# Filter tiles between kv tiles, and halves of filter tiles between gates, in the opening of a long-convolution and GeGLU kernel

## The chip, the cores and the metric

The kernel runs on one core of a Trainium2 chip. The metric is the device time of one execution in microseconds (us), lower is better. The engines are named as in the profile: PE is TensorE's matmul side and PEld its weight loads, DVE is VectorE, ACT is ScalarE, POOL is GpSimd and SP is SyncE, which here only issues DMAs.

## The reference

Two layers are applied twice in turn, A, B, A, B, to one sequence of 2048 tokens with 576 channels, in bfloat16. Layer A is a gated long convolution, layer B a gated feed-forward network of width 4608.

```
def A(q, k, v, shift_k, ssm_k, ssm_D):         # q is layernorm(x)
    k_shift = sum over t of k_pad[:, t:t+S] * shift_k[:, ks-1-t]      # 4 taps
    kv = k_shift * v
    y = irfft(rfft(kv, 2S) * rfft(ssm_k, 2S))[:S] + kv * ssm_D        # causal convolution, length 2048
    return q * y

def B(x, w_gate, w_up, w_down):                # x is layernorm(x)
    return (gelu(x @ w_gate) * (x @ w_up)) @ w_down

x = A_q
x = x + A(layernorm(x), ...);  x = x + B(layernorm(x), ...)
x = x + A(layernorm(x), ...);  x = x + B(layernorm(x), ...)
```

The convolution does not depend on x, so its result y is computed once and used by both A layers.

## The kernel before

**Tiling.** The sequence is cut into four blocks of 512 tokens, the channels stay together. Each block b of the filter `ssm_k` (transposed to time by channels, `hT[b]`) goes through a Fourier transform that is written as matmuls with the matrix `G`: four tiles `kt` of 128 frequencies, each with two halves `s` (cosine and sine). `h_tile(b, kt, pool)` makes one such tile: `fwd_h` runs eight matmuls of 128x288 per half into a PSUM tile, ScalarE evacuates it (L189), and the finished tile is spilled to DRAM (`Hd[b][kt]`, L266) by a DMA on POOL's queue. Block 1's tiles go to a resident tensor `H1`, and are spilled too. The kv blocks are transformed in the same way with the matrix `F1`: in the opening, `kfwd(kt)` makes the kv tile `kc[kt]` of block 0 (L198, L200), `kacc(kt)` multiplies it with block 0's filter tile on VectorE (L225 to L229), `pair0` adds and subtracts those products (L630), and `inv0(mt)` transforms back (L261), which gives `y[0]`.

**The opening** is the function `begin`: one order written out by hand for all engines, from the first DMA to the first gate/up matmul of the feed-forward network. After block 0's `inv0` it runs layer A's gate for the first 512 tokens, in four row groups j: `gate0(j)` is two VectorE operations (L801, L806), a small POOL operation for minus the mean (`nm`, L834) and a square with a sum on ScalarE (`junk`, L842); `root0(j)` makes 1/sqrt(variance) in two POOL operations (`ve` L849, `rstd` L850); `norm0(j)` writes the normalised tile xn on VectorE (L1017, L1019); `turn0(j)` transposes it with nine TensorE operations into PSUM (L1028); `copy0(j)` copies it to `xnT` on VectorE (L1036). Between these stand the remaining filter tiles of blocks 2 and 3, and `kv1_ops(n)`, VectorE's multiplies for block 1's kv.

**Queues and buffers in the opening.** The transposed filters `hT[b]` come by transposing DMAs on SP's queue (`load_h`, L495) into a pool of two buffers, so `load_h(3)` waits for the last reader of `hT[1]`, which is `h_tile(1, 3)`. On SP's queue the first two gate/up weight groups (`more(1)`, L760 to L762) stand ahead of `load_h(3)`, and the third (`more(2)`) behind it. POOL's queue carries the spills, the loads of k and v (`load_k`, `load_v`) and the small gate operations, in program order. A spill is not issued at once: `spill` puts it in a list, and `flush` issues what stands in the list, so a tile's spill goes out when the next tile is flushed. `ps()` hands out PSUM tiles: three buffers shared with the feed-forward network and with `turn0`, and every fourth time a buffer of its own.

**Behind the opening** an order worked out when the kernel is built interleaves everything else: gate/up matmuls (L1116), GeLU on ScalarE (L1120), the product hT on VectorE (L1121), down matmuls (L1132), and blocks 1 to 3 of the convolution in between. It does not depend on the order inside `begin`.

Of the kernel before, what the change touches and what calls it, by code (L numbers as in the profile page):

```python
# [14 lines left out]
BF16 = mybir.dt.bfloat16  # L15
# [3 lines left out]
P = 128  # L19
# [37 lines left out]
class Conv:  # L57
# [418 lines left out]
    def begin(self, gate0, root0, norm0, turn0, copy0, x0_stats, more, scratch, wide, stay):  # L476

        tc, nc, D = self.tc, self.nc, self.D
        with ExitStack() as es:
# [13 lines left out]
            def load_h(b):  # L493
                t = hp.tile([P, RT, D], BF16, tag="h", name="h")
                nc.sync.dma_start_transpose(out=t[:], in_=self.hk[:, b * BS:(b + 1) * BS])  # L495
                return t
# [22 lines left out]
            G = tmp.tile([P, RT, 2 * NFQ], BF16, name="G")  # L519
# [25 lines left out]
            hT = {0: hp.tile([P, RT, D], BF16, tag="h", name="h")}  # L545
# [14 lines left out]
            def f_angles(g):  # L560
# [4 lines left out]
                for i in range(2):  # L565
                    row = 2 * i if g == 2 else 2 * g + i
                    for s in range(2):
                        nc.scalar.activation(out=j4[:, i, s, :], in_=cv, func=ACT.Identity, bias=offs[:, s:s + 1],
                                             scale=rowf[:, row:row + 1])

            def h_tile(b, kt, pool):
                if b == 1:
                    t = self.H1[:, kt, :, :]
                else:
                    t = pool.tile([P, 2, D], BF16, tag="kr" if pool is self.krp else "hr", name="h0")
                for s in range(2):
                    self.fwd_h(G, hT[b], kt, s, t)
                self.flush(0.0)
                self.spill(self.Hd[b][kt], t)
                return t  # L580
            h0 = {}
            self.H1 = stay()
            kv0 = deque(self.kv_ops(0))
# [5 lines left out]
            for i in range(RT):  # L589
                h0[KTS[i]] = h_tile(0, KTS[i], self.hrp if i == 0 else self.krp)  # L590
                for _ in range(4):
                    kv0.popleft()[1]()
                if i == 1:
                    negate(0)
                if i < 2:
                    self.mask(jg[i])
                    self.sines(flat(Fs[i]), jg[i])
                if i < 1:
                    f_angles(i + 1)
                if i == 1:  # L600
                    more(0)
            hT[2] = load_h(2)
            h_tile(1, 0, self.hrp)
            more(1)
            h_tile(1, 2, self.hrp)
            self.load_k(1, nc.gpsimd)
            x0_stats(0)
# [4 lines left out]
            def kfwd(kt):  # L612
                kc[kt] = self.kcp.tile([P, 2, D], BF16, tag="kc", name="kc")
                for s in range(2):
                    self.fwd_full(self.vt_[0], neg, kt, s, kc[kt])
                self.flush(0.0)
                self.spill(self.Kd[0][kt], kc[kt])

            def kacc(kt):
                for part in range(2):  # L620
                    t = self.ybp.tile([P, D], BF16, tag="yb", name="yb")
                    self.prod(part, kc[kt], h0[kt], t[:])
                    A[(part, kt)] = t
# [3 lines left out]
            def pair0(kt, sg):  # L627
                for part in range(2):
                    b = self.ybp.tile([P, D], BF16, tag="yb", name="yb")
                    nc.vector.tensor_tensor(out=b[:], in0=A[(part, kt)][:], in1=A[(part, kt + 2)][:],  # L630
                                            op=ALU.subtract if sg else ALU.add)
                    self.yb[(part, kt, sg)] = b
# [6 lines left out]
            kfwd(2)  # L639
            kacc(0)  # L640
            self.mask(jg[2])
            kfwd(1)
            kacc(2)
            self.sines(flat(self.F2[:]), jg[2])
            pair0(0, 0)
            kfwd(3)
            kacc(1)
            self.load_v(1, nc.gpsimd)
            kacc(3)
            pair0(1, 0)  # L650
            nc.scalar.activation(out=warm[:], in_=self.pis[:, 1:2], func=ACT.Gelu_apprx_tanh)
            h_tile(1, 1, self.hrp)
            h_tile(1, 3, self.hrp)
            hT[3] = load_h(3)
            h_tile(2, 0, self.hrp)
            h_tile(2, 2, self.krp)
            inv0(0)
# [9 lines left out]
            def kv1_ops(n):  # L667
                for _ in range(n):
                    next(ops)[1]()
            gate0(0)  # L670
            gate0(2)
            root0(0)
            gate0(1)
            h_tile(2, 1, self.hrp)
            root0(2)
            norm0(0)
            h_tile(2, 3, self.krp)
            gate0(3)
            root0(1)
            turn0(0)  # L680
            norm0(2)
            copy0(0)
            root0(3)
            norm0(1)
            h_tile(3, 0, self.hrp)
            turn0(2)
            copy0(2)
            norm0(3)
            turn0(1)
            copy0(1)  # L690
            turn0(3)
            kv1_ops(2)
            copy0(3)
            h_tile(3, 2, self.krp)
            kv1_ops(6)
            h_tile(3, 1, self.hrp)
            h_tile(3, 3, self.krp)
# [523 lines left out]
```

## Time and profile before

| | |
|---|---|
| three runs | 942.17, 943.13, 943.75 us (median 943.13) |
| the profiled execution | 943.32 us; its span, first to last instruction, 941.5 us |
| busy, share of the span | PE 98%, PEld 57%, DVE 61%, ACT 31%, POOL 15% |
| granted TensorE clock | 1.00 |
| first gate/up matmul | 62.71 us |
| DMA | 127.46 MB, mean 135 GB/s |

The span is what the trace covers, from its first instruction to its last; the execution's own time holds 1.8 us more. All times inside the trace are counted from the span's start. In timelines a row gives the start, the length, the engine and line, the operation with its output and inputs, and how many such instructions are merged; in brackets how long the engine idled before it, and what ended that idle time. The length of a merged matmul row runs to the modelled end of its last matmul, so the distance from one row's start to the next one's is the better measure of a slot.

### The profile page before, as it was taken

How to read it: one execution, taken by the hardware profiler on the slowest of the kernel's cores; microseconds unless marked ns; L12 is line 12 of the kernel's file. 1: busy time of each engine (PE TensorE's matmuls, PEld its weight loads, DVE VectorE, ACT ScalarE, POOL GpSimd, SP SyncE). 2: the span in 40 equal slices, each digit the busy share in tenths (PEclk: the TensorE clock that was granted, in tenths of full speed). 3: DMA queues.
4: the chain of work that ended last, by engine and by line, in shares of the span. 5: the costliest groups of instructions: out<-in, count | busy, mean ns of one | idle time of the engine just before them, and what ended most of it. 6: DMA issues, size and time to landing. Idle time of an engine off the chain costs nothing.

```text
span 941.5 us, 19061 instructions
## 1 busy us (share of the span) xinstructions
PE 926.9 (98%) x8128; PEld 536.5 (57%) x8128; DVE 571.4 (61%) x1027; ACT 295.9 (31%) x541; POOL 143.2 (15%) x303
## 2 busy tenths in 40 slices
PE   7989999999999999999999999999999999999998
PEld 5755564665655646546546556556556556556555
DVE  8977887898898637988982333663333335523332
ACT  8846214432124334231222421441221223311211
POOL 2453100511123104230100100230000002100000
PEclk9999999999999999999999999999999999999999
DMA  7989986765953522983930630891630630797720
GB/s 184 323 238 274 293 183 148 133 162 142 226 190 64 113 77 52 195 212 87 221 107 2 133 94 26 136 156 39 129 99 1 129 98 14 135 206 155 147 65 26
DMA packets 129065, 127.46 MB, mean 135 GB/s; under 512 B 45587, under 2 KB 121684, under 8 KB 128980
## 3 DMA queue, kind: packets, MB, share of 16 engines
q1 hardware_dynamic: 119904, 90.85, 45.7%
q0 software_dynamic: 8944, 34.49, 11.4%
q8 instruction: 63, 1.03, 0.5%
q10 hardware_dynamic: 132, 0.91, 0.4%
q14 instruction: 22, 0.18, 0.1%
HBM read 105.58 MB, written 10.62 MB: 123 GB/s over the span
## 4 chain that ended last, share of the span: by engine, by line
PE 91%; DMA 3%; DVE 2%; POOL 2%; ACT 1%; issue 1%; SPq 0%; POOLq 0%; DVEq 0%
PE gu L1116 59%; PE dn L1132 27%; DMA h<-in_A_ssm_k_dram 2%; PE cps L208 1%; PE cps L261 1%; PE ps L187 1%; DMA k<-in_A_k_dram 1%; POOL rstd L850 1%; PE ps L198 1%; DVE x_c L1161 0%; PE cps L187 0%; POOL ve L849 0%; ACT junk L842 0%; DVE x_c L877 0%; DMA xnT<-xn 0%
## 5 line engine op out<-in xcount | busy, mean ns | idle before, releaser
L1116 PE MATMUL gu<-xnT,wgu 64*128 64x512 bf16 x5184 | 565.5, 376 | 2.1 <-DVE x_c L1161 1.0
L1116 PEld LDWEIGHTS <-wgu 64*128 64x128 bf16 x5184 | 254.3, 94 | 305.2 <-issue 10.1
L1120 ACT ACTIVATE ga<-gu 128x512 f32<-128x512 f32 x288 | 171.9, 597 | 549.9 <-PE gu L1116 541.1
L1121 DVE TENSOR_TENSOR hT<-ga,gu 128x512 bf16<-128x512 f32 x288 | 197.6, 686 | 221.2 <-ACT ga L1120 219.7
L1132 PE MATMUL dn<-wd,hT 128*128 128x288 bf16 x2304 | 291.0, 286 | 0.5 <-DVE ob L1141 0.5
L1132 PEld LDWEIGHTS <-hT 128*128 128x128 bf16 x2304 | 223.5, 98 | 66.1 <-issue 10.5
L1166 DVE TENSOR_TENSOR x_c<-x_c,dn 128x576 f32<-128x576 f32 x64 | 48.2, 753 | 82.3 <-PE dn L1132 82.0
L834 POOL TENSOR_SCALAR nm<-s 128x1 f32<-128x1 f32 x60 | 21.1, 352 | 344.1 <-DVE x_c L1161 215.1
L842 ACT ACTIVATE junk<-x_c,nm 128x576 bf16<-128x576 f32 x48 | 37.0, 771 | 40.8 <-POOL nm L834 40.8
L327 POOL DMA_DIRECT2D hr<-Hd x32 | 17.3, 541 | 161.2 <-DVE prod L228 161.2
L850 POOL TENSOR_TENSOR rstd<-ve,neghalf_t 128x1 f32<-128x1 f32 x60 | 39.9, 665 | 5.0
L229 DVE TENSOR_TENSOR sum<-prod 128x576 bf16<-128x576 bf16 x72 | 33.0, 458 | 2.5
L187 PEld LDWEIGHTS <-G 128*128 128x128 bf16 x256 | 25.5, 100 | 11.2 <-issue 2.2
L187 PE MATMUL ps<-h,G 128*128 128x288 bf16 x192 | 27.6, 298 | 2.5 <-DMA h<-in_A_ssm_k_dram 1.7
L1152 DVE TENSOR_TENSOR ob<-x_c,dn 128x576 bf16<-128x576 f32 x15 | 11.2, 753 | 27.2 <-PE dn L1132 19.0
L163 DVE TENSOR_TENSOR kvt<-k,skc 128x1152 bf16<-128x1152 bf16 x32 | 23.9, 754 | 0.5
L849 POOL TENSOR_SCALAR ve<-ss 128x1 f32<-128x1 f32 x60 | 18.1, 301 | 32.4 <-ACT junk L842 32.3
L216 DVE TENSOR_TENSOR kc<-eo 128x288 bf16<-128x288 f32 x48 | 19.2, 453 | 2.1 <-ACT eo L211 2.1
L877 DVE SCALAR_TENSOR_TENSOR x_c<-g_t,rstd,x_c 128x576 f32<-128x576 f32 x16 | 13.1, 818 | 12.0 <-POOL rstd L850 11.9
L211 ACT COPY eo<-cps 128x576 f32<-128x576 f32 x24 | 15.3, 636 | 15.2 <-PE cps L208 12.7
L269 POOL DMA_DIRECT2D out_dram<-ob x12 | 6.7, 555 | 86.3 <-DVE ob L1152 86.2
L383 DVE TENSOR_TENSOR zs<-sum 128x576 f32<-128x576 bf16 x24 | 18.1, 755 | 0.5
(112 smaller groups left out, 464.7 us busy)
## 6 DMA issues: line engine op xcount, KB each, us to landing
wgu<-in_B_w_gate_dram SPq DMA_DIRECT2D x45, 576.0 KB, 5.7
wd<-in_B_w_down_dram SPq DMA_DIRECT2D x30, 864.0 KB, 6.7
wgu<-in_B_w_up_dram SPq DMA_DIRECT2D x45, 512.0 KB, 8.2
hr<-Hd POOLq DMA_DIRECT2D x32, 288.0 KB, 5.3
kr<-Kd POOLq DMA_DIRECT2D x24, 288.0 KB, 5.4
Hd<-h POOLq DMA_DIRECT2D x12, 288.0 KB, 4.6
Kd<-kc POOLq DMA_DIRECT2D x12, 288.0 KB, 6.6
k<-in_A_k_dram POOLq DMA_DIRECT2D x3, 1008.0 KB, 6.1
```

The costliest lines, as they stand in the source:

```text
L163: nc.vector.tensor_tensor(out=st[dst][:], in0=self.kt_[b][:, s0:s0 + 2, :], in1=self.skc[:, j, :].unsqueeze(1).to_broadcast([P, 2, D]), op ...
L187: nc.tensor.matmul(ps[:, h, 0:HW], lhsT=G[:, i, s * NFQ + kt * P: s * NFQ + (kt + 1) * P], rhs=src[:, i, h * HW:(h + 1) * HW], start=(n == ...
L216: self.nc.vector.tensor_tensor(out=dst, in0=eo[:, 0, :], in1=eo[:, 1, :], op=op)
L229: nc.vector.tensor_tensor(out=dst, in0=pr[:, 0, :], in1=pr[:, 1, :], op=ALU.subtract if part == 0 else ALU.add)
L834: nc.gpsimd.tensor_scalar(out=v["nm"][:], in0=v["s"][:], scalar1=-1.0 / D, scalar2=None, op0=ALU.mult)
L842: nc.scalar.activation(out=junk[:], in_=get_x(), func=ACT.Square, bias=v["nm"][:, 0:1], accum_out=v["ss"][:])
L850: nc.gpsimd.tensor_tensor(out=v["rstd"][:], in0=ve[:], in1=neghalf_t[:, 0:1], op=ALU.pow)
L1116: nc.tensor.matmul(pair[:, s, :], lhsT=w[r0:r0 + HK, k, gi * P:(gi + 1) * P], rhs=xnT[r0:r0 + HK, b, :], start=(k == 0), stop=(k == NKC - 1))
L1120: nc.scalar.activation(out=ga[:], in_=pair[:, 0, :], func=ACT.Gelu_apprx_tanh)
L1121: nc.vector.tensor_tensor(out=hT[:, fi, :], in0=ga[:], in1=pair[:, 1, :], op=ALU.mult)
L1132: nc.tensor.matmul(acc[:, h, 0:HW], lhsT=hT[:, fi, j * P:(j + 1) * P], rhs=wd[2 * wb + fi // WT][:, fi % WT, h * HW:(h + 1) * HW], start=( ...
L1166: nc.vector.tensor_tensor(out=xh, in0=xh, in1=acc[:, :, 0:HW], op=ALU.add)
```

## The change

`h_tile` is split: `h_half` makes one half of a tile per call, and the second call also flushes the spill list and puts the tile in it. `h_tile` is two calls of it. In the order of the opening, three things move. Block 1's tiles (1,1) and (1,3) go from behind `kfwd(3)` to between block 0's kv tiles, and `load_h(3)` with them. Tiles (2,1), (2,3), (3,0) and (3,2) are cut in halves that are placed singly between the gate's steps, so that ScalarE's squares and evacuations come by turns. The last transposed tile, `turn0(3)`, comes behind both halves of (3,2), where it was ahead of them. No operation is added or taken away.

```diff
+            half = {}
+
+            def h_half(b, kt, pool):
+                s = 1 if (b, kt) in half else 0
+                if s == 0:
+                    half[(b, kt)] = self.H1[:, kt, :, :] if b == 1 else pool.tile(
+                        [P, 2, D], BF16, tag="kr" if pool is self.krp else "hr", name="h0")
+                t = half[(b, kt)]
+                self.fwd_h(G, hT[b], kt, s, t)
+                if s == 1:
+                    self.flush(0.0)
+                    self.spill(self.Hd[b][kt], t)
+                return t
+
             def h_tile(b, kt, pool):
...
+                h_half(b, kt, pool)
+                return h_half(b, kt, pool)
...
             self.mask(jg[2])
+            h_tile(1, 1, self.hrp)
             kfwd(1)
             kacc(2)
             self.sines(flat(self.F2[:]), jg[2])
             pair0(0, 0)
+            h_tile(1, 3, self.hrp)
+            hT[3] = load_h(3)
             kfwd(3)
             kacc(1)
             self.load_v(1, nc.gpsimd)
             kacc(3)
             pair0(1, 0)
             nc.scalar.activation(out=warm[:], in_=self.pis[:, 1:2], func=ACT.Gelu_apprx_tanh)
-            h_tile(1, 1, self.hrp)
-            h_tile(1, 3, self.hrp)
-            hT[3] = load_h(3)
             h_tile(2, 0, self.hrp)
             h_tile(2, 2, self.krp)
             inv0(0)
...
             gate0(0)
+            h_half(2, 1, self.hrp)
             gate0(2)
+            h_half(2, 1, self.hrp)
             root0(0)
+            h_half(2, 3, self.krp)
             gate0(1)
-            h_tile(2, 1, self.hrp)
             root0(2)
             norm0(0)
-            h_tile(2, 3, self.krp)
+            h_half(2, 3, self.krp)
+            turn0(0)
+            h_half(3, 0, self.hrp)
             gate0(3)
             root0(1)
-            turn0(0)
             norm0(2)
             copy0(0)
             root0(3)
             norm0(1)
-            h_tile(3, 0, self.hrp)
+            h_half(3, 0, self.hrp)
             turn0(2)
             copy0(2)
             norm0(3)
+            h_half(3, 2, self.krp)
             turn0(1)
             copy0(1)
+            h_half(3, 2, self.krp)
             turn0(3)
             kv1_ops(2)
             copy0(3)
-            h_tile(3, 2, self.krp)
             kv1_ops(6)
             h_tile(3, 1, self.hrp)
             h_tile(3, 3, self.krp)
```

More of the change, by code (lines that the diff above doesn't have):

```diff
@@ L569, in f_angles @@
                                              scale=rowf[:, row:row + 1])
-            def h_tile(b, kt, pool):
[L572 to L580, printed above, removed]
+            half = {}
[10 more added lines that the diff above has]
+                return t
+            def h_tile(b, kt, pool):
+                h_half(b, kt, pool)
+                return h_half(b, kt, pool)
             h0 = {}
```

## The prediction

> **What bounds the kernel now.** I read the page's busy rows first, then TensorE's timeline of the opening (0 to 63 us), the chain of waits, the DMA answers in stretches of 2 us, and last the timelines of ScalarE, VectorE and GpSimd (POOL).
>
> ```profile
> PE 926.9 (98%) x8128; PEld 536.5 (57%) x8128; DVE 571.4 (61%) x1027; ACT 295.9 (31%) x541; POOL 143.2 (15%) x303
> ```
>
> TensorE is busy for 926.9 of 941.5 us. An edit that leaves its work alone can only remove some of the 14.6 us of idle time. From 21.18 us to the first gate/up matmul at 62.71 TensorE idles in one place, shown in its timeline (start, length, line, idle before and releaser):
>
> ```profile
> 47.74 1.14 PE L187 MATMUL ps<-h,G 128*128 128x288 bf16 x8
> 49.86 0.66 PE L1028 MATMUL xps<-ident,xn 128*128 128x128 bf16 x9 [0.98 <-ACT h L189]
> 52.17 2.13 PE L187 MATMUL ps<-h,G 128*128 128x288 bf16 x16 [1.65 <-DMA h<-in_A_ssm_k_dram]
> 54.15 1.17 PE L1028 MATMUL xps<-ident,xn 128*128 128x128 bf16 x18
> 56.22 0.68 PE L1028 MATMUL xps<-ident,xn 128*128 128x128 bf16 x9 [0.90 <-DVE xn L1017]
> ```
>
> From start to start, eight matmuls of half a filter tile take 0.98 us and nine transposes 0.52. By these slots the gaps are 49.86 - 48.72 = 1.14, 52.17 - 50.38 = 1.79 and 56.22 - 55.19 = 1.03 us, 3.96 in all. The first waits for ScalarE to empty a PSUM tile, the second for block 3's transposed filter (hT[3]), the third for the normalised tile xn3. That is the most these edits can win. The chain of waits names the one that matters:
>
> ```profile
> 36.04 1.01 PE ps L187 x9
> 37.05 15.08 DMA h<-in_A_ssm_k_dram
> 52.13 0.05 issue
> 52.17 2.13 PE ps L187 x16
> ```
>
> The load is issued when tile (1,3)'s matmuls free its buffer and lands at 52.13. Why 15 us? Two DMA answers (queue, packets, MB, share of 16 engines), first 36 to 38 us, then 48 to 50:
>
> ```profile
> q0 software_dynamic: 172, 0.64, 80.5%
> q1 hardware_dynamic: 168, 0.17, 24.2%
> ```
> ```profile
> q1 hardware_dynamic: 1537, 0.40, 126.4%
> q0 software_dynamic: 2, 0.00, 0.6%
> ```
>
> q1 is SP's queue. At 36 to 38 its packets are 1 KB (0.17 MB in 168), so wgu's: the two weight loads issued at 22.9 to 33.2, the last piece landing at 48.7. POOL's q0 moves as many packets, but of nearly 4 KB. The 256-byte packets (0.40 MB in 1537) of the transposing load come in numbers only from 45 us, when q0 has emptied and the weights ahead of it are through. The DMA engines are full from 22 to 50 us (shares of 0.96 to 1.30 in every 2 us).
>
> **Tiles (1,1) and (1,3) move up.** No work is added: 32 matmuls, four evacuations, two spills go between kfwd(2), kfwd(1) and kfwd(3). kfwd(1) ends at 32.94 instead of 30.98, kfwd(3) at 36.86 instead of 32.94, and TensorE reaches inv0(0) at 40.8 as now. Who needs kc? VectorE is full from 21 to 48 us; it takes kacc(1) at 35.65 and kacc(3) at 38.05. With 0.53 us an evacuation and 1.05 for the sine, ScalarE now does H(1,1) from 30.82, kc1 at 32.16 and 33.14, the sine 33.68, H(1,3) 34.74 and 35.27, kc3 36.08 and 37.06 to 37.70. That is in time by 0.35 us; were it late, the hT[3] wait below would hide 2 us of it. The table load (1.28 us) slides to 37.7, tile (2,0)'s evacuations to 39.1 and 39.7, before inv0 needs their PSUM tiles at 40.8 and 41.8. Cost and gain: nothing.
>
> On POOL's queue the spill of (1,1) precedes kc1's, and (1,3)'s now stands ahead of load_v(1), which also waits for kfwd(3)'s last matmul: issue at 36.9, not 33.25. By its own 10.6 us it lands at 47.5; its user, the multiply that ends the first kv half, runs at 63.04. Hidden.
>
> **hT[3] is issued earlier.** Its buffer is free at 35.1, 1.96 us sooner. If landing followed issue it would be 50.2. I take 52.1, unchanged, by the nearest row: q1 still holds 0.9 MB of weights ahead of it (what it moves from 35 to 45 us), q0 gets as many packets as q1 and four times the bytes, and the bytes that both must move first are the same ones in another order. The other two transposing loads say the same: one issued at 4.40 had its packets only from 10 us, as q0 and ScalarE's queue emptied (landing after 11.6 us); one at 20.65 on empty queues landed after 5.4. Bounds: 50.2 below; above, 54.4, if it has to wait for load_v's landing at 47.5 instead of starting at 45.3.
>
> The Trainium skill, "DMA: Bandwidth & Descriptors", section "Queues, rings and completion order", says that each DMA engine goes round its queues packet by packet and takes one ring's descriptors in order. The 172 against 168 packets agree. It speaks against this edit: by it the landing stays, by the issue time alone the sum would be 3.0 us instead of 1.0.
>
> **Halves between the gates.** ScalarE's order becomes square 0, half, square 2, two halves, square 1, half, half of (3,0), square 3. Now the first half of (2,1) is evacuated from 46.32 (after square 0 at 45.54, 0.78), not at 49.18, so the 0.98 wait goes. Next is xn0. POOL has one thing more ahead of root 0: flush in (2,1)'s second half issues the spill of (2,2), 0.62 us, which was behind it. rstd 0 ends at 48.17 + 0.62 = 48.8, xn0 at 49.6, the transposes run 49.6 to 50.15. This gain only lengthens the wait for hT[3] to 2.0 us: worth 0 with landing at 52.13.
>
> After that TensorE runs, by slots: (3,0) 52.17 to 54.13, turn0(2) to 54.65, a half of (3,2) to 55.63, turn0(1) to 56.15, the other half to 57.13, turn0(3), (3,1) and (3,3) 4.44 more to 61.57. The 1.03 us for xn3 is gone because 1.96 us of (3,2) stand ahead of it.
>
> But square 3, now at 52.06, is queued behind the evacuation of (3,0)'s first half (53.37, 0.53): 53.90. With the present distances ve follows 0.96 later, 54.86, rstd ends 1.10 later, 55.96, xn3 is complete at 56.80, 0.33 before its transposes. With the slowest pair of POOL rows (ve 2 to rstd 2, 2.04 us) it is 57.75 and 0.62 is lost. I take the quick pair: the slow one ran beside VectorE's gate multiplies, and here VectorE copies from PSUM. copy0(3), after copy0(1), two kv operations and its 0.82, ends at 59.7, needed at 61.67. VectorE ends its kv operations at 64.4; the first hT multiply is due at 64.5. The loop behind keeps its order, and its weights have 8 us and more (the down weights' issue at 62.91 and 13.4 us, first use 89.4).
>
> **Sum.** The first gate/up matmul comes at 61.57 + 0.09 (now 56.74 + 5.88 + 0.09 = 62.71) = 61.67: 1.04 us sooner. The span of 941.5 becomes 940.5; the execution (943.32, 1.8 outside the span) 942.3. The median of the runs shown, 943.13, is 0.19 below that execution: 942.1.
>
> **Rivals.**
> *The load lands with its issue, 50.2.* (3,0) follows turn0(0) at once, then xn1 (53.6), xn3 (55.2) are each in time to 0.1 us, and gate/up starts at 59.7: 3.0 us, 940.1. For it: 2 us more of overlap for a load whose queue instruction lasts 10.72 us. Against: the packet rows above. Any landing 0.85 us earlier gives 1.9 or more.
>
> *The load lands later: slower.* load_v's 0.59 MB leaves q0's work at 33 us and enters at 36.9. If q0 runs short in between and packets of 256 B starve while it moves 4 KB ones, the transposes start at load_v's landing, 47.5, not 45.3: landing 54.4, 1.2 us slower, 944.3. With the next larger load's 12.5 us (k, from 24.83) instead of 10.6 it is 3.1, 946.2. The turning point is a landing at 53.2; past 55.1 it shows. Against: at 36 us q0 would have been given k's 1.03 MB and six tiles of 0.295 since 24.8, and moved 1.6 of it (its MB from 26 to 36 us): 1.2 MB are left, 3.7 us at 0.32 MB per us, and load_v comes within 1.
>
> *TensorE's clock drops in the one long gap.* Idle pieces of at most 1.65 us become one of 2.0. If the 32 matmuls of (3,0) and (3,2) ran at half speed they would cost 3.9 us more: 946.0. Against: from 48.72 to 52.17 TensorE already works only one slot of 0.52, with a granted clock of 1.00 in 50 to 54 us.
> The Trainium skill's "TensorE: Matmul & The Clock Gate", "Part 1: The HAM clock gate", wants an idle window of about 3.4 us; by that it should not happen here.
>
> *It only shuffles:* xn3 late, landing half a microsecond off either way: 0 to 0.4 us gained, 942.7 to 943.1.
>
> **Chances.** Landing kept or mere shuffling: 0.49. Load earlier: 0.30. Load later: 0.16, of which 0.11 past 55.1. Clock, or a late kc3 beyond its cover: 0.05. About 0.2% (1.9 us) is what a measurement of this kernel can tell from no change; so faster is 0.30, same 0.49 + 0.05 = 0.54, slower 0.11 + 0.05 = 0.16. The likeliest case alone is 941.3 to 943.1. The range takes in the early landing and the late one at its first price, and leaves out the 0.16: 940.0 to 944.4.
>
> **What would show it.** Right: one TensorE gap of about 2 us ahead of (3,0), ended by the transposing load near 52.1 although issued at 35.1; none before turn0(3); no gap before 48.7; first gate/up matmul near 61.7. Wrong: landing well before 51.3 or after 53.2, kacc(3) waiting for kc3, a gap before turn0(3) from rstd, clock below 1.00 after 52 us.

## The result and the profile after

The changed kernel is slower: 945.82 us, median of 7 runs (944.04 to 947.82), against 942.79 for the kernel before (7 runs, 941.48 to 943.75). The ratio is 1.0035, 95% interval 1.0024 to 1.0046, so 2.3 to 4.3 us. The profiled execution took 947.82 us with a span of 946.0 us. TensorE's busy time hardly moved:

```profile
PE 927.5 (98%) x8128; PEld 536.7 (57%) x8128; DVE 571.4 (60%) x1027; ACT 296.4 (31%) x541; POOL 142.2 (15%) x303
```

Everything is in the opening. TensorE's timeline of the changed kernel, in the columns used before:

```profile
49.88 1.14 PE L187 MATMUL ps<-h,G 128*128 128x288 bf16 x8
51.26 0.68 PE L1040 MATMUL xps<-ident,xn 128*128 128x128 bf16 x9 [0.24 <-DVE xn L1029]
56.37 3.50 PE L187 MATMUL ps<-h,G 128*128 128x288 bf16 x16 [4.43 <-DMA h<-in_A_ssm_k_dram]
59.70 0.67 PE L1040 MATMUL xps<-ident,xn 128*128 128x128 bf16 x9
60.21 1.14 PE L187 MATMUL cps<-h,G 128*128 128x288 bf16 x8
61.19 0.67 PE L1040 MATMUL xps<-ident,xn 128*128 128x128 bf16 x9
61.69 1.14 PE L187 MATMUL ps<-h,G 128*128 128x288 bf16 x8
62.67 0.67 PE L1040 MATMUL xps<-ident,xn 128*128 128x128 bf16 x9
63.17 2.12 PE L187 MATMUL ps<-h,G 128*128 128x288 bf16 x16
...
67.19 1.04 PE L1128 MATMUL gu<-xnT,wgu 64*128 64x512 bf16 x8
```

Three things are to be seen. The wait for ScalarE ahead of turn0(0) and the wait for xn3 ahead of turn0(3) are gone, as planned. The wait for block 3's transposed filter grew from 1.65 to 4.43 us. And the 16 matmuls behind it take 59.70 - 56.37 = 3.33 us instead of 1.96. The chain of waits of the changed kernel gives the load's time from issue to landing:

```profile
37.30 0.03 PE cps L198
37.33 18.99 DMA h<-in_A_ssm_k_dram
56.32 0.05 issue
56.37 3.50 PE ps L187 x16
```

It took 18.99 us, against 15.08 before. Absolute times need care here: in this execution block 0's first kv tile, kfwd(0), starts at 27.34, in the one before at 25.10. The change touches nothing ahead of it, and over the profiles of this case it starts between 24.5 and 28.0. So from here on, times in the opening are counted **from the first kv tile's start**, and called "relative".

| relative, us | before | after |
|---|---|---|
| load of hT[3] issued | 11.95 | 9.99 |
| it lands | 27.03 | 28.98 |
| first gate/up matmul | 37.61 | 39.85 |

The first gate/up matmul is 2.24 us later: the landing 1.95 later, the 16 matmuls 1.37 longer, the xn3 wait of 1.03 gone, which makes 2.29. The two traces differ by 2.24 us here, the medians by 3.0; what the rest is was not found. The slow matmuls are the clock, as the busy time by stretches of the changed kernel shows (stretch, length, then the busy time and count of PE, PEld, DVE, ACT and POOL, and behind them the granted clock, the DMA share and GB/s):

```profile
54.00:56.00 2.00, 0.00 (x0) 0.00 (x0) 1.20 (x4) 0.00 (x0) 0.42 (x1) 0.94 1.13 236
56.00:58.00 2.00, 1.63 (x7) 1.04 (x8) 0.00 (x0) 0.00 (x0) 0.00 (x0) 0.50 1.13 217
58.00:60.00 2.00, 2.00 (x16) 1.44 (x15) 0.00 (x0) 1.50 (x4) 0.00 (x1) 0.70 1.02 280
60.00:62.00 2.00, 2.00 (x27) 1.75 (x25) 1.56 (x5) 1.17 (x2) 1.86 (x4) 1.00 0.08 27
```

After the long gap the granted clock is 0.50 and comes back within 4 us. All 7 runs of the changed kernel have a mean clock below 1.00 (0.996 or 0.998). (Disturbed executions are left out of the ratios; the profiled one of experiment e was such a one, so of e only the runs are used.)

Why does the load land late? The DMA answers of the changed kernel (queue, packets, MB, share of 16 engines) for 36 to 38 us and, while the transposes run, for 50 to 52 us:

```profile
q0 software_dynamic: 59, 0.28, 54.5%
q1 hardware_dynamic: 206, 0.20, 47.6%
```
```profile
q1 hardware_dynamic: 818, 0.21, 112.6%
q0 software_dynamic: 22, 0.08, 18.1%
```

In the first stretch POOL's queue (q0) moves 0.28 MB; in the same relative stretch before, 34 to 36 us, it moved 0.56. That does not decide the landing: kernel l, below, has the same order of DMAs, its q0 moves 0.57 MB in that stretch (36 to 38 us, relative 9 to 11), and its load lands as late:

```profile
q0 software_dynamic: 129, 0.57, 76.1%
```

The second stretch, relative 22.7 to 24.7, is the one to compare with 48 to 50 us before, relative 22.9 to 24.9. Here 22 packets of POOL's queue lie among the 256-byte packets of the transposing load, and only 818 of those pass in 2 us; before, 2 lay among them and 1537 passed. By the shares of 16 engines, one transposing packet took 44 ns here and 26 ns before. What is still on its way on POOL's queue is the spill of tile (2,0), with (2,2)'s, issued at 49.05, behind it. The rows of the DMAs whose queue instructions run at 42.8 us, where (2,0)'s spill is issued, show size and time to landing:

```profile
Hd<-h POOLq DMA_DIRECT2D x1, 288.0 KB, 10.0
h<-in_A_ssm_k_dram SPq DMA_TRANSPOSE x1, 19.0
```

Before, that spill took 8.7 us. Both the spill and the load became slower at the same time. The spill is issued at relative 15.49 (before 14.96), and the fiftieth 256-byte packet of the load starts at 19.5 (before 20.2): the two have come closer by 1.2 us.

### The profile page after: what moved, and what is told of

It is laid out like the page before. It is cut to its first block, busy times and chain, and to the rows that moved or that the text cites. A ratio compares the mean times of both kernels' runs of the same rounds, so it can differ in the third digit from the quotient of the medians.

```text
span 946.0 us, 19062 instructions
## 1 busy us (share of the span) xinstructions
PE 927.5 (98%) x8128; PEld 536.7 (57%) x8128; DVE 571.4 (60%) x1027; ACT 296.4 (31%) x541; POOL 142.2 (15%) x303
## 3 DMA queue, kind: packets, MB, share of 16 engines
q8 instruction: 63, 1.03, 0.5%
## 4 chain that ended last, share of the span: by engine, by line
PE 91%; DMA 3%; DVE 2%; POOL 2%; ACT 1%; issue 1%; SPq 0%; DVEq 0%
PE gu L1128 58%; PE dn L1144 27%; DMA h<-in_A_ssm_k_dram 2%; PE ps L187 2%; PE cps L208 1%; PE cps L261 1%; POOL rstd L862 1%; DMA hn<-in_A_ssm_k_dram 1%; DVE x_c L1173 0%; PE ps L198 0%; POOL ve L861 0%; ACT junk L854 0%; DVE x_c L889 0%; PE cps L187 0%; DMA xnT<-xn 0%
## 5 line engine op out<-in xcount | busy, mean ns | idle before, releaser
L1144 PEld LDWEIGHTS <-hT 128*128 128x128 bf16 x2304 | 223.6, 98 | 66.1 <-issue 10.5
L187 PE MATMUL ps<-h,G 128*128 128x288 bf16 x200 | 29.6, 303 | 5.2 <-DMA h<-in_A_ssm_k_dram 4.4
L1164 DVE TENSOR_TENSOR ob<-x_c,dn 128x576 bf16<-128x576 f32 x15 | 11.2, 754 | 27.0 <-PE dn L1144 19.0
L163 DVE TENSOR_TENSOR kvt<-k,skc 128x1152 bf16<-128x1152 bf16 x32 | 23.9, 753 | 0.4
```

Source lines behind the costliest of these rows:

```text
L163: nc.vector.tensor_tensor(out=st[dst][:], in0=self.kt_[b][:, s0:s0 + 2, :], in1=self.skc[:, j, :].unsqueeze(1).to_broadcast([P, 2, D]), op ...
L187: nc.tensor.matmul(ps[:, h, 0:HW], lhsT=G[:, i, s * NFQ + kt * P: s * NFQ + (kt + 1) * P], rhs=src[:, i, h * HW:(h + 1) * HW], start=(n == ...
L1144: nc.tensor.matmul(acc[:, h, 0:HW], lhsT=hT[:, fi, j * P:(j + 1) * P], rhs=wd[2 * wb + fi // WT][:, fi % WT, h * HW:(h + 1) * HW], start=( ...
```

## The experiments

The theories, numbered as the expectations name them: (1) the load of v, pushed back on POOL's queue, delays the transposing load; (2) the transposing load is slowed by its own earlier issue; (3) the halves between the gates do it, by way of (2,2)'s earlier spill; (4) it is the order of POOL's queue, whatever the issue; (5) a copy of POOL's queue that is still under way when the transposes start slows both; (6) that copy is (2,0)'s spill. Each kernel was run beside the kernel before on the same chip; "lowered" counts the runs with a mean granted clock of 0.998 or less. One profile's landing differs by about 1 us from another's of like kernels, so smaller differences are not read. "late" stands where (2,0)'s spill is issued behind the load. The kernel before has lowered runs too, in these comparisons 27 of 110 (4 of 29, 6 of 31, 9 of 31, 8 of 19), with medians 2.6 to 3.2 us above its others. None of them was traced, and the medians and ratios in the table hold them.

| kernel | median, us (before's) | ratio, 95% | landing, relative | gate/up, relative | (2,0)'s spill, us | lowered |
|---|---|---|---|---|---|---|
| a: tiles and load only | 946.41 (943.23) | 1.0025, 1.0008 to 1.0042 | 28.30 | 40.15 | 10.4 | 6 of 8 |
| b: halves only | 941.95 (943.23) | 0.9993, 0.9973 to 1.0013 | 26.04 | 35.54 | 7.5 | 3 of 10 |
| c: after, v later still | 943.35 (943.23) | 0.9999, 0.9981 to 1.0018 | 28.39 | 39.23 | 11.4 | 4 of 10 |
| d: after, hT[3] early | 941.11 (943.23) | 0.9977, 0.9966 to 0.9988 | no wait | 34.65 | 6.8 | 0 of 10 |
| e: after, load held | 946.15 (943.26) | 1.0029, 1.0009 to 1.0049 | - | - | - | 8 of 9 |
| f: before, load sooner | 941.84 (943.26) | 0.9993, 0.9978 to 1.0007 | 25.5 | 36.46 | 6.9 | 0 of 10 |
| g: before, hT[3] early | 943.25 (943.26) | 0.9991, 0.9977 to 1.0005 | no wait | 36.46 | 6.4 | 0 of 10 |
| h: halves, hT[3] early | 940.83 (943.26) | 0.9974, 0.9961 to 0.9987 | no wait | 34.74 | 7.0 | 0 of 10 |
| i: before, spill (2,0) late | 943.30 (943.78) | 0.9994, 0.9981 to 1.0008 | 26.13 | 36.71 | 4.9 | 0 of 10 |
| j: after, both spills late | 940.99 (943.78) | 0.9979, 0.9967 to 0.9991 | 25.24 | 34.74 | late | 0 of 10 |
| k: j, and v later | 941.43 (943.78) | 0.9974, 0.9962 to 0.9986 | 22.9 | 34.58 | late | 1 of 10 |
| l: after, gap filled | 944.64 (943.78) | 1.0013, 0.9998 to 1.0028 | 29.35 | 38.84 | 10.5 | 1 of 10 |
| m: after, spill (2,0) late | 941.04 (943.64) | 0.9968, 0.9953 to 0.9983 | 25.67 | 35.18 | late | 0 of 10 |
| n: after, spill (2,2) late | 945.55 (943.64) | 1.0023, 1.0007 to 1.0039 | 27.73 | 38.53 | 9.4 | 10 of 10 |
| o: before, v later | 957.01 (943.64) | 1.0125, 1.0093 to 1.0157 | 42.2 | 54.55 | 23.4 | 4 of 4 |

**Which part: a, b, c.** Kernel a keeps the tiles' move and puts the gates back as they were.

```diff
             gate0(0)
-            h_half(2, 1, self.hrp)
             gate0(2)
-            h_half(2, 1, self.hrp)
             root0(0)
-            h_half(2, 3, self.krp)
             gate0(1)
+            h_tile(2, 1, self.hrp)
...
```

> Only tiles (1,1), (1,3) and hT[3]'s load move up; the gate's steps and tiles stand as before. Times against 942.8 us before and 945.8 after. Theory 1 (moving the tiles pushes the load of v and its 0.59 MB later in POOL's queue, into the time of the transposing load): landing about 2 us later than before, counted from the first kv tile's start, a TensorE gap of over 3 us, granted clock near 0.5 behind it, the 0.9 us gap for xn3 still there: 946 us. Theory 2 (issuing the transposing load earlier, on full queues, makes it itself slower): the same, 946. Theory 3 (the harm comes from the halves between the gates, whose spill of (2,2) goes out earlier): landing as before, 942.8.

Kernel b is the other part alone, with block 1's tiles and the load back in their old place.

```diff
-            h_tile(1, 1, self.hrp)
             kfwd(1)
...
-            h_tile(1, 3, self.hrp)
-            hT[3] = load_h(3)
             kfwd(3)
...
+            h_tile(1, 1, self.hrp)
+            h_tile(1, 3, self.hrp)
+            hT[3] = load_h(3)
             h_tile(2, 0, self.hrp)
```

> Only the gate's halves move; tiles (1,1), (1,3), hT[3]'s load and the load of v stand as before. Theories 1 and 2: landing as before (about 27 us after the first kv tile's start), one gap of 2.0 us, no gap for xn3, 1.0 us faster than before: 941.8; if 2.0 us of idle time are enough to lower the clock, some 1.4 us dearer, 943.2. Theory 3: landing 2 us later, clock lowered, 945.8.

The whole loss is in a, and b loses nothing. b's TensorE timeline has only the wait for the load left:

```profile
52.63 2.13 PE L187 MATMUL ps<-h,G 128*128 128x288 bf16 x16 [1.40 <-DMA h<-in_A_ssm_k_dram]
```

Theory 3 falls. Kernel c takes the changed kernel and puts the load of v behind root0(2), out of the transposing load's time.

```diff
-            self.load_v(1, nc.gpsimd)
...
             root0(2)
+            self.load_v(1, nc.gpsimd)
```

> The changed kernel with one line moved: the load of v for block 1 is issued behind root 2 of the gate (about 49 us) and no longer ahead of kacc(3) (37 us). Theory 1: the software queue empties some 1.9 us sooner (0.59 MB at 0.32 MB per us), hT[3] lands at 50 to 52 us or about 25 to 27 after the first kv tile's start, the gap is 2 us or less, clock 1.00: 940 to 942. Theory 2: the load still takes 17 to 19 us from its issue, gap over 4 us, clock 0.5 behind it: 945.8. Theory 3: as theory 2. In every theory v lands about 58 to 60, just ahead of its use at 63.

The median is back at the kernel before, so moving v helps. But it is no cure: 4 of 10 runs are lowered (median 945.6; the other six 942.0). The profiled run is one of the four: its load lands at 28.39 without v, and (2,0)'s spill took 11.4 us. Theory 1, in which v alone delays the load, falls; where the load lands in the other six runs is not known.

**Is it the issue time: e, f.** Kernel e keeps all of the change, but a one-element VectorE copy that reads hT[1] behind kacc(1) holds the load's issue back to about relative 13 by the forecast, later than before (11.95).

```diff
             kfwd(3)
             kacc(1)
+            nc.vector.tensor_copy(out=held[:], in_=hT[1][0:1, 0, 0:1])
+            hT[3] = load_h(3)
```

> The changed kernel, but hT[3]'s load is held back: a one-element VectorE copy (about 0.06 us) reads hT[1] behind kacc(1), so that the load's buffer is free 13 us after the first kv tile's start, where it was 10 in the changed kernel and 12 before. The tiles and POOL's queue stay as changed. Theory 2 (the earlier issue makes the load itself slower): landing 26 to 27 us after the first kv tile's start, gap of about 2 us, clock 1.00 in most runs: 942. Theory 4 (the order of the spills and loads on POOL's queue, not the issue, makes it late): landing 28 to 29, gap over 4, clock 0.5 behind it: 945.8.

It stayed slow: ratio 1.0029 (1.0009 to 1.0049), with 8 of its 9 runs lowered. Kernel f does the reverse: the old order, with the load issued at 33.62 us (relative 7.8) into room of its own in a scratch tile.

```diff
+            hT[3] = neg[:, 2:2 + RT, :]
+            nc.sync.dma_start_transpose(out=hT[3], in_=self.hk[:, 3 * BS:4 * BS])
...
-            hT[3] = load_h(3)
```

> The kernel before, with a place of its own for hT[3], its load issued as soon as SP has passed on the first two weight groups (about 33 us, 8 after the first kv tile's start, where it is 12). Nothing else moves. Theory 2: the load lands later than before by 2 us or more (29 to 31 after the first kv tile's start), clock lowered behind the gap: 946 or more. Theory 4, and the prediction's ring order: landing 27, 943.2. If landing followed the issue: 23 to 24, no wait for it, 941.5.

The load landed at relative 25.5, 1.5 us sooner for 4.1 us of earlier issue, TensorE did not wait for it, and the kernel was not slower. Theory 2 expected the opposite in both and falls: issuing late does not cure the change, and issuing early does not bring it on.

**What an early landing is worth: d, g, h.** The same scratch room, but the load is issued right behind block 1's, where both queues are still short; in the changed kernel (d), in the one before (g) and in b's (h).

```diff
             hT[1] = load_h(1)
+            hT[3] = neg[:, 2:2 + RT, :]
+            nc.sync.dma_start_transpose(out=hT[3], in_=self.hk[:, 3 * BS:4 * BS])
...
-            hT[3] = load_h(3)
```

> The changed kernel with a place of its own for hT[3], so that its load is issued behind hT[1]'s at about 13 us, when the queues are nearly empty, instead of waiting for tile (1,3). All theories that put the loss on the landing of hT[3]: landing about 20 us, no TensorE gap ahead of (3,0), none longer than 1 us in 45 to 63, clock 1.00 throughout: 3 us faster than before, 939.8. If the load instead delays hT[2], the weights or x by its 3 us of DMA time, that part is given back. If the time was lost elsewhere: 945.8.

> The kernel before, with a place of its own for hT[3] and its load issued behind hT[1]'s at about 13 us; nothing else moves. The wait for the load goes, the waits for ScalarE (about 1 us) and for xn3 (about 1 us and what xn1 adds) stay: 1 us faster than before by the trace's distances, 942.2; clock 1.00 in every run.

> Only the gate's halves move, and hT[3] has a place of its own, loaded behind hT[1] at about 13 us; tiles (1,1) and (1,3) stand as before. If moving those tiles is worth nothing by itself, the same as the changed kernel with the early load, 940 to 941, 2 to 3 us faster than before, clock 1.00 in every run; if the earlier tiles do help, 1 us slower than that.

With the wait out of the way the change gains 0.0023 of the time (d), and the halves alone gain the same (h): gate/up at relative 34.65 and 34.74. So moving tiles (1,1) and (1,3) is worth nothing by itself. g alone is worth about what was expected, 1 us: gate/up comes 1.15 us sooner, and the ratio of 0.9991 has an interval that also holds no change. Without the halves, ScalarE and xn3 are still waited for.

**The copy under way: i, j, k.** Kernel j is the changed kernel with the spills of (2,0) and (2,2) held until behind root0(1).

```diff
-                    self.spill(self.Hd[b][kt], t)
+                    if (b, kt) in hold:
+                        late.append((self.Hd[b][kt], t))
+                    else:
+                        self.spill(self.Hd[b][kt], t)
...
+            def issue_late():
+                for dst, t in late:
+                    nc.gpsimd.dma_start(out=dst, in_=t[:].rearrange("p s d -> p (s d)"))
+            hold, late = [(2, 0), (2, 2)], []
...
             root0(1)
+            issue_late()
```

> The changed kernel with the spills of (2,0) and (2,2) held until root 1 of the gate has been issued (about 27 us after the first kv tile's start). Theory 5: only the load of v and one kv spill still overlap the first packets of the transposes: landing 26.5 to 28, clock 1.00 in at least half of the runs, 942 to 943.5. Theory 4 in any other form (the bytes moved later on POOL's queue by the tiles): landing 28.5 to 29, 945.8.

Kernel k adds c's edit, the late v, to it.

> The same, and the load of v is issued behind root 2 as in the run with the late v. Theory 5: POOL's queue is empty when the transposes start; landing 25 to 26.5 us after the first kv tile's start, gap of 2 us or less, clock 1.00 in nearly all runs, 940.5 to 941.5, as with the early load of hT[3]. If the transposes are slow for another reason: landing 28, 943 or more, as the late v alone.

Kernel i asks whether a spill can bring the delay on in the old order: (2,0)'s spill is issued behind the first `nm`, at 48.15 us, while the transposes run.

```diff
+            hold, late = [(2, 0)], []
...
             gate0(0)
+            issue_late()
```

> The kernel before with one DMA moved: the spill of tile (2,0), 0.29 MB, is issued behind the gate's first nm (about 20 us after the first kv tile's start) instead of 15 us after it, so that it falls on the transposing load's packets, which start about 20. Theory 5 (a software-queue transfer still under way when the transposes start slows both): landing 29 us after the first kv tile's start or later, clock lowered behind the gap in most runs, 945 to 946. Theory 1 in its first form (bytes on POOL's queue are served first, so only the sum ahead counts): 0.29 MB less ahead of it, landing 26 to 27, 942 to 943.

j and k cure it, and both have ratios below 1; j lands sooner than was expected of it. k's load lands 11.2 us after its issue (relative 11.63), with neither v nor block 2's spills around. i missed theory 5's expectation: nothing was slowed. But it does not test the theory, for its spill's data moved only at 51 to 52 us, when the transposing packets were nearly through. Whether the spill waits for the transposes is not shown: in h, where the transposing load has long landed, (2,2)'s spill is issued at 46.27 and its data moves only from about 50 us; from 47 to 49 POOL's queue has no line there either:

```profile
q1 hardware_dynamic: 428, 0.42, 112.4%
```

**Which spill: m, n.** j's edit with one tile in `hold`, (2,0) in m and (2,2) in n.

```diff
-            hold, late = [(2, 0), (2, 2)], []
+            hold, late = [(2, 0)], []          # m;  n: [(2, 2)]
```

> The changed kernel with only the spill of (2,0) held until root 1 of the gate; the spill of (2,2) goes out as in the changed kernel. Theory 6 (the spill of (2,0), still under way on POOL's queue when the first transposing packets come, is what makes the load crawl): as with both held, landing 25 to 26 us after the first kv tile's start, clock 1.00 in nearly all runs, 941. If the spill of (2,2) is the one, or both count: landing 28 or more, 943 to 946.

> The changed kernel with only the spill of (2,2) held until root 1; the spill of (2,0) goes out as in the changed kernel. Theory 6: landing 28 to 29.5, clock lowered in most runs, 945 to 946, like the changed kernel. If (2,2)'s spill is the one: 941.

TensorE's timeline of m:

```profile
51.43 0.68 PE L1049 MATMUL xps<-ident,xn 128*128 128x128 bf16 x9 [0.23 <-DVE xn L1038]
53.24 2.13 PE L187 MATMUL ps<-h,G 128*128 128x288 bf16 x16 [1.13 <-DMA h<-in_A_ssm_k_dram]
55.21 0.67 PE L1049 MATMUL xps<-ident,xn 128*128 128x128 bf16 x9
```

and of n:

```profile
54.76 3.44 PE L187 MATMUL ps<-h,G 128*128 128x288 bf16 x16 [3.46 <-DMA h<-in_A_ssm_k_dram]
```

Holding the one DMA of 288 KB turns the change from 1.0035 into 0.9968; holding the other leaves it at 1.0023 with every run lowered. In m's DMA answer for 48 to 50 us POOL's queue has no line at all (1019 packets, the weights' last pieces among them):

```profile
q1 hardware_dynamic: 1019, 0.29, 119.0%
```

Theory 6 stands. Two more rows show that the slowing goes both ways. The same spill, issued at the same relative time in the changed order, took 10.0 us beside the load and 6.8 in d, where the load had landed before; the load took 18.99 us beside the spill and 15.7 in m. And it is more than the spill's bytes: its 0.29 MB is 0.9 us at the 0.32 MB per us that POOL's queue moved at 36 to 38 us before, and m's load lands 3.3 us sooner than the changed kernel's.

**Does a gap in POOL's queue bring it on by itself: o.** The old order, with only `load_v` moved behind tile (1,3), to relative 13.2.

```diff
-            self.load_v(1, nc.gpsimd)
             kacc(3)
...
             h_tile(1, 3, self.hrp)
+            self.load_v(1, nc.gpsimd)
```

> The kernel before with one line moved: the load of v is issued behind tile (1,3), about 13 us after the first kv tile's start (12 in the changed kernel, 8 before), so that it and the spills of (1,3) and (2,0) behind it are later on POOL's queue; tiles and hT[3]'s load stand as before. If this displacement alone is enough to push (2,0)'s spill into the transposes: landing 28 to 29.5, clock lowered in most runs, 945. If the tiles' earlier place is needed too (it also lets the weights on SP's queue, and so the transposes, come earlier): landing 27, 943.2.

The kernel became 13.4 us slower, far past what either side expected. From the chain of waits and TensorE's timeline of o:

```profile
36.98 30.22 DMA h<-in_A_ssm_k_dram
```
```profile
49.78 0.66 PE L1028 MATMUL xps<-ident,xn 128*128 128x128 bf16 x9 [0.98 <-ACT h L189]
67.24 3.93 PE L187 MATMUL ps<-h,G 128*128 128x288 bf16 x16 [16.80 <-DMA h<-in_A_ssm_k_dram]
```

and its DMA answer for 48 to 50 us:

```profile
q1 hardware_dynamic: 213, 0.05, 70.7%
q0 software_dynamic: 50, 0.19, 64.2%
```

POOL's queue was dry from 40 to 42 us, the weights got through, and the transposes began then, over 3 us sooner in relative time than before. v and three spills, all issued ahead of the first transposing packets, came in among them, and all of it crawled: 213 packets of the transposing load in 2 us, v in 23.7 us, the spills in 21.2 to 23.9. From the issue of (2,0)'s spill to the fiftieth packet of the load it is 5.1 to 5.4 us in the kernel before, b and f, 3.0 to 4.3 in the changed kernel, a, c, l and n, and 1.8 in o; the closer the two are, the longer this spill takes from group to group.

**The clock's share: l.** The changed kernel with 24 useless matmuls (overwritten, 2.9 us) between turn0(0) and (3,0), so that TensorE is not idle for long.

```diff
+        for _ in range(24 if fill is not None else 0):
+            nc.tensor.matmul(ps[:, 0, 0:HW], lhsT=G[:, 0, 0:P], rhs=fill[:, 0, 0:HW], start=True, stop=True)
```

> The changed kernel with 24 matmuls of no use (2.9 us, written over by the next ones) between the first transposed tile and (3,0), so that TensorE works while it waits. If the lowered clock is a price of its own for the idle stretch: clock 1.000 in all runs, the first 16 matmuls behind the wait take 1.96 us by their starts and not 3.33, landing as in the changed kernel, 1.4 us faster than it: 944.4. If the clock falls for another reason, 945.8 or more.

TensorE's timeline of l, and its stretch from 56 to 58 us:

```profile
51.40 3.10 PE L186 MATMUL ps<-h,G 128*128 128x288 bf16 x24
56.38 2.12 PE L189 MATMUL ps<-h,G 128*128 128x288 bf16 x16 [1.87 <-DMA h<-in_A_ssm_k_dram]
58.34 0.67 PE L1042 MATMUL xps<-ident,xn 128*128 128x128 bf16 x9
```
```profile
56.00:58.00 2.00, 1.62 (x14) 1.29 (x14) 0.00 (x0) 0.44 (x1) 0.00 (x0) 1.00 1.08 275
```

The landing is as late as in the changed kernel (relative 29.35), the clock stays at 1.00, the 16 matmuls take 1.96 us, and the ratio is 1.0013 instead of 1.0035. So the clock is a price of its own: 1.37 us by the profile. By the two ratios it is 2 us, but their intervals overlap.

How long an idle stretch must be is not fixed by this. In k's profile the clock fell early in the opening, behind a wait for ScalarE of 2.06 us, long before the load is waited for:

```profile
19.34 2.08 PE L187 MATMUL cps<-h,G 128*128 128x288 bf16 x8 [2.06 <-ACT h L189]
```
```profile
20.00:22.00 2.00, 2.00 (x10) 1.29 (x9) 1.93 (x4) 2.00 (x4) 0.55 (x1) 0.50 0.38 147
```

So a lowered run does not by itself tell that the load was late.

## Why the prediction was wrong

**The step that failed** is "hT[3] is issued earlier ... I take 52.1, unchanged". In relative times the load landed 1.95 us later, not level. The reason given, that "the bytes that both must move first are the same ones in another order", leaves out what the order decides: which copy is under way when the transposing packets come. In the changed kernel the transposes began some 0.7 us earlier in relative time, and (2,0)'s spill, issued 0.53 us later and behind the late v, was still on its way. The two then slowed each other. m shows that this spill decides it; c and o show that v's place has a share, o that a late v alone is enough to start it. How the delay divides among the spill's own later issue, v's place and the transposes' earlier start was not separated, nor why they start earlier.

**The rival "the load lands later"** had the direction. In the times of the profile before, the landing is 28.98 + 25.10 = 54.1, and the rival's first price had 54.4; that this is close is luck. Its condition, POOL's queue running short near 36 us, is not what decided (l does not have it), and the transposes did not wait for v: their fiftieth packet starts at relative 19.5, v lands at 20.2, 45.3 in the times of the profile before and not 47.5. What it lacked is that the load's own packets become slower: in o the load took 30.22 us although its packets were moving from 41 to 42 on. The price it had, 1.2 us, also leaves out the clock.

**The clock rival** was priced apart from the late landing, on a gap of 2 us; here the two come together. In the profiles, idle stretches of 3.03 us (a), 3.46 (n) and 4.43 (after) were followed by granted clocks of 0.50 to 0.51, and one of 2.06 (k) too; the wait of 1.87 in l and shorter ones were not. At 2.0 us the prediction left at most 0.05 for it; k's row says that it could have happened there. The Trainium skill, "TensorE: Matmul & The Clock Gate", "Part 1: The HAM clock gate", puts the idle window near 3.4 us and lets it run free of the kernel. The stretches of 3.46 and 4.43 fit that; k's and a's are shorter, so less than a whole idle window was enough here. The prediction's price was too high: 16 matmuls lost 1.37 us, where it had 3.9 for 32.

**The rule of the Trainium skill** that was used for the landing ("DMA: Bandwidth & Descriptors", "Queues, rings and completion order", queues served in turn, packet by packet) fits weights against spills, 168 to 172 packets. For the transposes the rows give 818 to 22, and no run here shows what sets that share.

**What held.** kacc(3) came at 40.28, 38.05 plus the 2.23 of the later start, so kc3 was in time. Tiles (1,1) and (1,3) are worth nothing by themselves (d against h). The halves take away the waits for ScalarE and for xn3: b's gate/up comes 2.07 us sooner, of which 0.99 is its earlier landing and the rest, 1.08, answers to the 1.04 of the sum; its median gain of 1.28 is inside an interval that also holds zero. turn0(0) starts at 51.26, relative 23.92, which is 49.0 in the times of the profile before, where 49.6 was forecast. And the early landing, forecast as worth 3.0 us, moved gate/up by 2.87 to 2.96 us in d, h and j, 2.0 to 2.5 by their ratios.

**A better version.** Holding (2,0)'s spill (m), or giving hT[3] early room of its own (d, h), gives ratios of 0.9968, 0.9977 and 0.9974, where the changed kernel has 1.0035. The intervals overlap, so which of them is best stays open. Part of the gain is that none of their 30 runs is lowered; against the runs of the kernel before that are not lowered, their medians are 1.6 to 2.0 us lower. The kernel before may pay for the spill too: m's load lands 1.4 us sooner than its own, little more than profiles differ by.

## What to carry to other kernels

A moved step is not free because the bytes stay the same: follow each queue to the moment when a transposing load reaches its head, and see which copies of the other queue will then be under way. If one will be, issue it later, behind the transposes, or load the transposed data earlier, while the queues are empty. Price a longer TensorE gap twice, once for its length and once more for the half clock that may follow it: here it followed stretches of 3 us and more, and in one profile one of 2.06.

## What the hardware showed

A transposing load and a copy that was issued ahead of its first packets slow each other far beyond their sizes. The load took 11.2 us from issue to landing without v or block 2's spills around (k), 15.08 in the kernel before, 18.99 after the change and 30.22 in o. The spill of (2,0), 288 KB, took 6.4 to 7.0 us where the load had landed before (d, g, h), 6.9 to 8.7 in b, f and the kernel before, 9.4 to 11.4 in the changed kernel, a, c, l and n, and 23.4 in o. The packets themselves take longer. By the shares of 16 engines shown above, a transposing packet took 26 ns in the kernel before (48 to 50 us), 44 after the change and 106 in o. A POOL packet of nearly 4 KB took 150 ns beside weights (before, 36 to 38 us), 263 after the change and 411 in o. What in the DMA engines makes them slow was not found.
